# Softmax reciprocals as a power of minus one on GpSimd, and history copies on GpSimd, in a two-branch attention kernel

**The chip, the cores and the metric.** One core of one Trainium2 chip. The metric is the device time of the whole kernel in microseconds (us), the median of several executions; lower is better.

## The reference

Two attention branches share x (1 x 2048 x 640; 32 heads of 20). A is full softmax attention, B looks at a window of 8 positions two apart (its own and 7 earlier ones); a sigmoid gate mixes them. Cut to what matters:

```python
def _A_ref(x, wqkv, wo):            # full attention; B_ref is alike, over a window of 8 positions, 2 apart
    ...
    scores = jnp.einsum("bhqd,bhkd->bhqk", q, k) * scale
    p = _softmax(scores, axis=-1)
    o = jnp.einsum("bhqk,bhkd->bhqd", p, v)
    ...
g = _sigmoid((x * gate_w).sum(-1, keepdims=True))
return g * a + (1 - g) * b
```

## The kernel before

A runs in 32 groups (4 blocks of 512 queries, 8 sets of 4 heads). In each, TensorE makes score tiles, ScalarE takes the exponential of most of them (`ebuf`), and VectorE approximates it for the rest by integer arithmetic (`uD`, then shifted copies `eD` that TensorE weighs with `vS`). TensorE sums both into the PSUM bank `obank`; one row for each head holds the softmax denominator. At the end of a group the result is normalised:

```python
def gen_norm(g):
    qc, q = GROUPS[g]
    T("dve", dvc(512), lambda e: e.transpose(oTt[:, :], obank[:, :]), reads=["obank"], writes=["oTt"])
    while not done.get(("gate", qc)):
        yield ("cond",)
    yield ("dve",)
    T("dve", 0.25, lambda e: e.reciprocal(rcp[:, :], oTt[:, 0:512:32]), reads=["oTt"], writes=["rcp"])
    en, c1, c2 = ("dve", 0.12, dvc(512)) if g == NG - 1 else ("pool", 0.24, 1.08)
    T(en, c1, lambda e: e.tensor_tensor(rcp[:, :], rcp[:, :], gA[qc % 2][:, :], ALU.mult), ...)
    ...
    T(en, c2, lambda e: e.tensor_tensor(oo, ii, ib, ALU.mult), reads=["rcp", "oTt"], writes=["oN0"])
    yield ("dve", DVE_AHEAD, max(sch.ready("oN0"), sch.free("oN1")))
    T("dve", dvc(256), lambda e: e.transpose(oN[1]..., oN[0]...), reads=["oN0"], writes=["oN1"])
    if g < NG - 1:
        ... # small DMAs: oTd <- oN1, which a later output product reads
```

`T(engine, cost, instruction, ...)` enters an instruction into a scheduler that runs **while the kernel is built**. It keeps a clock for each engine, adds the cost given (in us), and so decides in which order the instructions stand on each engine; `yield` lets other work go first until the moment asked for. A table `PLAN` of some fifty rows of constants steers these decisions. Each engine of the chip is given its instructions in that order.

In branch B, k and v are kept with 16 columns of history ahead of them, copied from the end of the chunk before (`TB` enters VectorE work and adds it to B's progress):

```python
TB(0.15, lambda e, bb=bb: e.tensor_copy(bb[:, :, 0:PADB], bb[:, :, TOK:TOK + PADB]), reads=[key], writes=[key], port=True)
```

## Time and profile before

| | before |
|---|---|
| median time | 836.07 us (835.97 to 836.23, 3 runs) |
| ScalarE busy | 803.9 of 835.4 us |
| ScalarE idle: ends / inside its stream of exponentials | 22 / 9.5 us |
| TensorE busy / VectorE busy / GpSimd busy | 789.3 / 683.7 / 138.7 us |
| VectorE's waits for oN (the product made on GpSimd) | 4.6 us in 6 |

The prediction shows the lines that these come from, but for the last:

```profile
DVE oN L772 <- POOL oN L770: 4.6, 6, 1.4
```

One more view of the kernel before: the timeline of VectorE and GpSimd at one normalisation (start, duration, engine, line, operation, in us).

```profile
404.47 0.70 DVE L758 STREAM_TRANSPOSE oTt<-obank 128x512 f32<-128x512 f32 x1
405.21 0.25 DVE L762 RECIPROCAL rcp<-oTt 128x16 f32<-128x16 f32 x1
...
405.54 0.23 POOL L764 TENSOR_TENSOR rcp<-rcp,gA 128x16 f32<-128x16 f32 x1 [23.07 <-DVE rcp L762]
405.85 1.05 POOL L770 TENSOR_TENSOR oN<-oTt,rcp 128x512 bf16<-128x512 f32 x1
...
407.58 0.44 DVE L772 STREAM_TRANSPOSE oN<-oN 128x256 f32<-128x256 f32 x1
```

The path from the end of the first transpose (405.17) to the end of oN (406.90) is 1.73 us. The second transpose starts at 407.58 without waiting, 0.68 us later: the order has three other VectorE instructions ahead of it. Over all 31 places the kept trace gives 0.10 to 3.1 us between the end of oN and the second transpose, with a median of 0.67.

### The profile page before, as it was taken

What the parts mean: (1) busy time and instruction counts of PE and PEld (TensorE: products, weight loads), DVE (VectorE), ACT (ScalarE), POOL (GpSimd) and SP (SyncE); (2) the same over time, 40 slices, a digit from 0 to 9 for tenths busy, and PEclk for the clock granted to TensorE, in tenths of its full rate; (3) what the DMA queues carried; (4) which work ended last, traced back from release to release, by engine and by line L of the source; (5) the groups of instructions that cost most, each with busy time, mean ns of one, the idle gap of its engine ahead of it and who ended that gap; (6) DMA issues with size and microseconds to landing.
All of it is one profiled execution on the core that took longest, in us unless ns stands there. A gap on an engine that the chain in (4) does not pass through costs nothing.

```text
span 835.4 us, 29602 instructions
## 1 busy us (share of the span) xinstructions
PE 789.3 (94%) x12599; PEld 289.9 (35%) x12601; DVE 683.7 (82%) x1205; ACT 803.9 (96%) x767; POOL 138.7 (17%) x180
## 2 busy tenths in 40 slices
PE   8999999999999899989998999999999999998997
PEld 4333323334333332333233333333333333333223
DVE  7567888889888887978797988798898898887873
ACT  4999999999999999999999999999999999999994
POOL 5013013431111111011111011111102111101110
PEclk9999999999999999999999999999999999999999
DMA  9112112200111110011001011110011001101100
GB/s 313 30 37 44 33 25 45 73 13 19 29 37 29 29 30 20 7 42 32 20 18 41 18 20 29 36 42 9 5 39 30 10 20 25 38 6 31 32 6 34
DMA packets 45016, 29.15 MB, mean 35 GB/s; under 512 B 27204, under 2 KB 43684, under 8 KB 44884
## 3 DMA queue, kind: packets, MB, share of 16 engines
q1 hardware_dynamic: 44596, 26.92, 12.4%
q8 instruction: 100, 1.64, 0.8%
q10 hardware_dynamic: 288, 0.33, 0.1%
q14 instruction: 32, 0.26, 0.1%
HBM read 11.94 MB, written 2.62 MB: 17 GB/s over the span
## 4 chain that ended last, share of the span: by engine, by line
PE 54%; ACT 30%; issue 10%; DVE 5%; DVEq 0%; ACTq 0%
ACT ebuf L1538 30%; PE score L1515 17%; PE obank L1583 13%; PE side L557 13%; PE score L557 5%; PE obank L1604 2%; DVE uD L1528 1%; PE side L1604 1%; DVE eD L797 1%; PE obank L459 1%; PE score L1230 1%; PE side L885 1%; DVE stage L869 0%; PE score L1604 0%; DVE stage L970 0%
## 5 line engine op out<-in xcount | busy, mean ns | idle before, releaser
L1538 ACT ACTIVATE ebuf<-score 128x1024 bf16<-128x1024 f32 (+1 forms) x735 | 792.6, 1237 | 11.6 <-PE score L1515 9.7
L1515 PE MATMUL score<-qT,kT 32*128 32x512 bf16 x2048 | 291.9, 384 | 31.6 <-ACT ebuf L1538 20.6
L1528 DVE TENSOR_SCALAR uD<-score 128x512 int16<-128x512 f32 x324 | 217.2, 683 | 38.4 <-PE score L1515 36.1
L797 DVE TENSOR_SCALAR eD<-uD 128x2048 int16<-128x2048 int16 x243 | 168.1, 722 | 7.9 <-PE obank L1583 7.2
L1515 PEld LDWEIGHTS score<-qT,kT 32*128 32x128 bf16 x2048 | 75.1, 91 | 282.7 <-ACT ebuf L1538 137.6
L1583 PE MATMUL obank<-ebuf,vA 128*21 128x512 bf16 x1724 | 161.3, 385 | 2.2 <-ACT ebuf L1538 1.8
L789 POOL TENSOR_TENSOR vS<-vA,vw 128x252 bf16<-128x252 bf16 x81 | 61.0, 757 | 291.5 <-PE obank L1583 256.3
L557 PE MATMUL side<-xT,kvw 128*32 128x256 bf16 (+1 forms) x2530 | 103.0, 281 | 3.1 <-DVE qkvB L853 1.4
L1583 PE MATMUL obank<-eD,vS 128*21 128x512 bf16 x972 | 84.1, 382 | 0.0
L557 PEld LDWEIGHTS side<-xT,kvw 128*32 128x32 bf16 x2530 | 59.3, 96 | 37.9 <-issue 22.0
L764 POOL TENSOR_TENSOR rcp<-rcp,gA 128x16 f32<-128x16 f32 x31 | 11.3, 365 | 351.9 <-DVE rcp L762 351.9
L1583 PEld LDWEIGHTS obank<-ebuf,vA 128*21 128x21 bf16 x1724 | 38.6, 89 | 82.3 <-issue 69.5
L970 DVE TENSOR_TENSOR stage<-qkvB,repB 128x1280 bf16<-128x1280 bf16 x64 | 52.9, 856 | 0.7 <-DMA repB<-eB 0.7
L869 DVE TENSOR_TENSOR stage<-qkvB 128x1280 bf16<-128x1280 bf16 x64 | 51.4, 830 | 0.1
L853 DVE CAST qkvB<-side 128x512 bf16<-128x512 f32 (+1 forms) x72 | 41.9, 591 | 10.5 <-PE side L557 10.5
L557 PE MATMUL side<-stage,ident 128*32 128x512 bf16 (+1 forms) x736 | 47.4, 345 | 1.2 <-DVE uD L744 0.5
L1604 PE MATMUL obank<-xT,zero 128*32 128x512 bf16 x444 | 37.9, 385 | 0.0
L770 POOL TENSOR_TENSOR oN<-oTt,rcp 128x512 bf16<-128x512 f32 x31 | 33.0, 1065 | 2.4
L1583 PE MATMUL obank<-uD,vA 128*21 128x512 bf16 x324 | 31.7, 382 | 0.0
L758 DVE STREAM_TRANSPOSE oTt<-obank 128x512 f32<-128x512 f32 x32 | 22.7, 709 | 9.0 <-PE obank L1583 8.9
L1583 PEld LDWEIGHTS obank<-eD,vS 128*21 128x21 bf16 x972 | 24.0, 92 | 17.4 <-issue 4.1
L557 PE MATMUL side<-woA_d,oTd 128*32 128x128 bf16 (+1 forms) x580 | 28.8, 293 | 0.0
(173 smaller groups left out, 555.5 us busy)
## 6 DMA issues: line engine op xcount, KB each, us to landing
repB<-eB SPq DMA_DIRECT2D x128, 32.0 KB
WqP<-in_A_wqkv_dram SPq DMA_DIRECT2D x16, 160.0 KB
stage<-in_B_wqkv_dram SPq DMA_DIRECT2D x1, 2400.0 KB
oTd<-oN SPq DMA_DIRECT2D x108, 20.0 KB
qT<-dst SPq DMA_DIRECT2D x104, 20.0 KB
out_dram<-outsb SPq DMA_DIRECT2D x12, 160.0 KB
kvw<-in_A_wqkv_dram SPq DMA_DIRECT2D x2, 800.0 KB
oTd<-in_A_x_dram SPq DMA_DIRECT2D x2, 640.0 KB
```

What stands on the lines that cost most here:

```text
L557: ins = e.matmul(o[j:k, :], l(j) if callable(l) else l[:, j:k], r, start=(first and i == 0), stop=(last and i == n - 1), skip_group_check= ...
L770: T(en, c2, lambda e: e.tensor_tensor(oo, ii, ib, ALU.mult), reads=["rcp", "oTt"], writes=["oN0"])
L789: T("pool", 0.7, lambda e: e.tensor_tensor(vS[:, d % 2, :, :], _ap(vA, (kb * NQ + q) * 4 * DV, [[0, K - 1], [1, 4 * DV]]), _ap(vw, 0, [[1, ...
L797: T("dve", 0.11 + 0.1334 * n, lambda e, k=k, sl=sl: e.tensor_scalar(eD[:, sl % NS, 0:512 * n].bitcast(I16), uD[d % 2][:, 0:512 * n].bitcas ...
L853: t = TB(dvc(n * TOK), lambda e, o=o, i=i: e.tensor_copy(o, i), reads=[("side", b)], writes=[key])
L869: TB(dvc(CN * TOK, 2), lambda e, w=w, ks=ks: e.tensor_tensor(prodB(w), qB[:, :, :], ks, ALU.mult), reads=["qB", "kB"], writes=[("prod", w) ...
L970: TB(dvc(CN * TOK, 2), lambda e, w=w, vs=vs, rr=rr: e.tensor_tensor(prodB(w), vs, rr, ALU.mult), reads=["vB", ("repB", w4 % NR)], writes=[ ...
L1515: ins = e.matmul(o, kT[32 * j:32 * j + 32, q, kb * P:(kb + 1) * P], qT[g % NQT][32 * j:32 * j + 32, :], start=True, stop=True)
L1528: t = T("dve", 0.69, lambda e: e.tensor_scalar(uD[d % 2][:, 512 * i:512 * (i + 1)].bitcast(I16), side[x], UOFF, 0.0, op0=ALU.add, op1=ALU. ...
L1538: exps[s] = T("act", actc(512 * n), lambda e: e.activation(ebuf[s % NE][:, 0:512 * n], score[s % 2][:, 0:512 * n], ACTF.Exp, scale=LN2 / S ...
L1583: ins = e.matmul(obank[32 * j:32 * j + DV, :], v, src, start=(kb == 0), stop=(last and k >= len(lst) - 4), skip_group_check=True)
L1604: ins = e.matmul(o[32 * j:32 * j + 32, :], w[:, 32 * j:32 * j + 32] if best else w[:, :], xT[:, 0, 0:512], start=bool(best), stop=bool(bes ...
```

## The change

The change takes work off VectorE: 31 of 32 reciprocals become a power with exponent -1 on GpSimd, ahead of the gate's product that was there already, and the 14 history copies go to GpSimd. `PLAN` is replaced by another table, and `BALL`, the total against which B's progress is measured, is lowered by 2. The diff, with all but the first of the 49 old and 54 new rows of the table cut:

```diff
 PLAN = {
-    0: ((0.34, 0.64), 0.37, 6.3, 2.5, 0.51, -1.0, -0.1, 11.8, 4.5, 7.2, 0.52, 0.47, 4.4, 1.86, 0.0, 0.85, 2, 0.0),
+    0: ((0.3, 0.64), 0.32, 2.5, 2.5, 0.49, -1.0, -0.1, 11.8, 7.0, 7.2, 0.51, 0.34, 4.4, 4.0, 0.0, 0.81, 2, 0.0),
 ... (all other rows: cut)
+    minus1 = sb([P, 1], FP32, "minus1")
...
+        T("dve", 0.06, lambda e: e.memset(minus1[:, :], -1.0), writes=["minus1"])
...
-        yield ("dve",)
-        T("dve", 0.25, lambda e: e.reciprocal(rcp[:, :], oTt[:, 0:512:32]), reads=["oTt"], writes=["rcp"])
+        if g == NG - 1:
+            yield ("dve",)
+            T("dve", 0.25, lambda e: e.reciprocal(rcp[:, :], oTt[:, 0:512:32]), reads=["oTt"], writes=["rcp"])
+        else:
+            T("pool", 0.8, lambda e: e.tensor_tensor(rcp[:, :], oTt[:, 0:512:32], _ap(minus1, 0, [[0, 16]]), ALU.pow),
+              reads=["oTt", "minus1"], writes=["rcp"])
...
-                TB(0.15, lambda e, bb=bb: e.tensor_copy(bb[:, :, 0:PADB], bb[:, :, TOK:TOK + PADB]), reads=[key], writes=[key], port=True)
+                T("pool", 0.3, lambda e, bb=bb: e.tensor_copy(bb[:, :, 0:PADB], bb[:, :, TOK:TOK + PADB]), reads=[key], writes=[key])
...
-    BALL = 172.0
+    BALL = 170.0
```

## The prediction

> **What bounds the kernel now.** I read the page first (busy times), then the ScalarE groups by form, the ScalarE part of the waits, and the ScalarE timeline at the two ends.
>
> Busy times and the chain of the page:
>
> ```profile
> PE 789.3 (94%) x12599; PEld 289.9 (35%) x12601; DVE 683.7 (82%) x1205; ACT 803.9 (96%) x767; POOL 138.7 (17%) x180
> ...
> PE 54%; ACT 30%; issue 10%; DVE 5%; DVEq 0%; ACTq 0%
> ```
>
> ScalarE (ACT) is busy 803.9 of 835.4 us, so it is idle for only 31.5 us in the whole run. TensorE's 94% is softer than it looks. The kernel puts in matmuls that compute nothing, where the build-time scheduler sees TensorE idle: line 1604, 444 of them into obank and 304 more into the other banks, 748 in all. They run four at a time, so they make 187 slots of about 0.215 us (the spacing of such slots in the timeline), some 40 us of work that could be left out. VectorE (DVE), which the change relieves, has 152 us of idle time and holds 5% of the chain.
>
> ScalarE's groups by form, and who ended its waits:
>
> ```profile
> L1538 ACT ACTIVATE ebuf<-score 128x1024 bf16<-128x1024 f32 x479 | 463.4, 1082 | 6.4 <-PE score L1515 5.0
> L1538 ACT ACTIVATE ebuf<-score 128x1536 bf16<-128x1536 f32 x255 | 359.2, 1530 | 5.1 <-PE score L1515 4.4 <-ACT ebuf L1538 0.2
> ```
> ```profile
> ACT ebuf L1538 <- PE score L1515: 9.7, 24, 2.1
> ACT stage L1082 <- PE score L1063: 6.9, 1, 6.9
> ACT xT L1243 <- PE score L1230: 6.3, 3, 4.4
> ```
>
> The exponentials of A's scores fill ScalarE. The reader is to see how little it waits in that stream: 9.7 us in 24 waits, all for score tiles from TensorE. The rest of its idle time lies at the ends. The timeline shows both: the first exponential starts at 19.62, the last starts at 823.22 and takes 0.60, and the end follows from 823.8 to 835.4 without an exponential.
>
> ```profile
> 19.62 1.45 ACT L1538 ACTIVATE ebuf<-score 128x1536 bf16<-128x1536 f32 x1 [2.10 <-PE score L1515]
> ...
> 823.22 0.60 ACT L1538 ACTIVATE ebuf<-score 128x512 bf16<-128x512 f32 x1 [0.18 <-PE score L1515]
> ...
> 830.75 1.08 ACT L1082 ACTIVATE stage<-score 128x512 bf16<-128x512 f32 x2 [6.93 <-PE score L1063]
> ```
>
> Up to 19.62 ScalarE works about 8.1 us and idles 11.5. After 823.8 it works 1.1 and idles 10.5. So 22 of the 31.5 idle us are the fixed ends, and **9.5 us is the idle time inside the stream**. That 9.5 us is all that a lighter VectorE can win.
>
> **What the Trainium skill says.** (1) "SBUF — State Buffer", section "SBUF: two separate sides": GpSimd and VectorE share one port pair as an exclusive lock; a VectorE instruction in a two-port mode, or with two SBUF inputs against a GpSimd one that reads SBUF, and a GpSimd instruction shut each other out for a whole instruction. The trace agrees: vS on GpSimd takes 598 to 1191 ns, and the VectorE eD instruction 627 to 1860. (2) "GPSIMD Engine Reference", section "Engine selection": elementwise work is about twice as slow there for two inputs. The trace has the same two steps on both engines: 128x16 multiply 222 ns (GpSimd, undisturbed) against 175, and the scaling of oN 1052 against 751; so 1.3 to 1.4 here. (3) "VectorE: DVE Perf Modes", section "Walkthrough: the 8-slice pipeline in each mode": VectorE's reciprocal is an iterated hardware divide, not a plain stream. The trace: 243 ns for 128x16, 68 more than the multiply of the same shape. No page that I found gives the cost of a power on GpSimd, and no row of this trace has one.
>
> **The change, part by part.**
>
> ```profile
> L758 DVE STREAM_TRANSPOSE oTt<-obank 128x512 f32<-128x512 f32 x32 | 22.7, 709 | 9.0 <-PE obank L1583 8.9
> L762 DVE RECIPROCAL rcp<-oTt 128x16 f32<-128x16 f32 x32 | 7.8, 243 | 0.4
> L840 DVE COPY qkvB<-qkvB 128x80 bf16<-128x80 bf16 x14 | 2.4, 173 | 0.1
> L764 POOL TENSOR_TENSOR rcp<-rcp,gA 128x16 f32<-128x16 f32 x31 | 11.3, 365 | 351.9 <-DVE rcp L762 351.9
> L770 POOL TENSOR_TENSOR oN<-oTt,rcp 128x512 bf16<-128x512 f32 x31 | 33.0, 1065 | 2.4
> ```
>
> *Removed from VectorE:* 31 of 32 reciprocals, 31 x 0.243 = 7.5 us, and all 14 history copies, 2.4 us: 9.9 us together. The gate's product was on GpSimd before already; what moves is the reciprocal ahead of it.
>
> *Added on GpSimd:* 31 powers and 14 copies. The scheduler's own entries for GpSimd (0.24 for the product, 1.08 for oN, 0.7 for vS) are close to what the trace has (0.222, 1.052, 0.610), so its entries for the new steps are probably measured too: 0.8 and 0.3. That is 31 x 0.8 + 14 x 0.3 = 29 us more, 138.7 to about 167 of 835: no bound. The path from oTt to oN grows: at 405 us of the timeline it is 0.25 (reciprocal) + 0.08 + 0.23 + 0.08 + 1.05; the power puts 0.8 where 0.25 was, so oN is 0.6 us later. The transpose that uses it is placed by the scheduler, which counts on this, so little of it should be waited for.
>
> *Given back through the lock:* two-port and two-input VectorE instructions start 243 + 64 + 64 times in 835 us, 0.45 per us. A power of 0.8 us meets 0.36 of them and holds each back by half its length at most on average: 31 x 0.36 x 0.4 = 4.5 us of VectorE time, an estimate, and the copies add 14 x 0.13 x 0.15, nothing. So of 9.9 us some 5.5 stays won.
>
> *The whole order is made anew.* This is the larger part. A table of scheduling constants is replaced, and the listings of the two built programs differ almost everywhere. Counts in them: exponentials of 1024 go 479 to 472, of 1536 from 255 to 261; score tiles that VectorE converts (uD) 324 to 320, the shifts eD 243 to 240; matmuls that compute nothing 748 to 804, so 14 more slots. The relief of VectorE was thus not spent on taking work from ScalarE: four more score tiles go through ScalarE. By the busy share of one (463.4/479 = 0.967 and 359.2/255 = 1.409 us, overlaps counted once) that is 6 x 1.409 - 7 x 0.967 = **+1.7 us of ScalarE**. VectorE gets 4 x 0.67 + 3 x 0.69 = 4.7 us less in addition. The listings of the first instructions and of the last (final tiles, output products, four final adds) are alike but for small shifts, so the 22 us of the ends stay.
>
> *Sum:* time = ends and other ScalarE work as before + 1.7 + the stream's idle time. With the stream's idle time unchanged at 9.5 that is 836.1 + 1.7 = 837.8. With none left it would be 828.3. How much of it goes? The waits of TensorE show what held the score tiles up:
>
> ```profile
> PEld score L1515 <- DVE uD L1528: 24.4, 53, 0.9
> PEld score L1515 <- DVE eD L797: 12.4, 32, 0.6
> PEld score L1515 <- DVE oTt L758: 4.3, 7, 0.9
> PEld score L1515 <- DVE rcp L762: 3.5, 7, 0.8
> ```
>
> VectorE is what TensorE waited for after ScalarE itself (137.6 us, which is harmless), and TensorE seldom lets ScalarE run dry: some of the ScalarE gaps that I opened in the timeline (305.77, 458.42) have score matmuls delayed by a run of obank work, others (452.67, 692.37, 715.51) follow a run of VectorE evacuations. About 45% of 9.5 us, 4.3 us, is my choice: a lighter VectorE, and an order that was tuned for it. That gives 837.8 - 4.3 = **833.5 us**.
>
> **Rivals.** *(a) The saving is hidden and the new order costs.* VectorE is not the bound, so nothing is won, and 1.7 us of ScalarE comes on top: 837.8, or up to 842 if the new order fits the chip less well than the old one. For it: 5% of VectorE in the chain, and the count of exponentials went up. Against: an order worse than the old one would hardly have been kept. *(b) A new wait on GpSimd.* The power takes 2 us, not 0.8; oN then comes 1.2 us late 31 times and VectorE, which works in order, waits for it. Before there is a trace of it: "DVE oN L772 <- POOL oN L770: 4.6, 6". Up to 31 x 1.2 = 37 us of VectorE waiting, against 152 us of idle time; a quarter of it reaching ScalarE makes 845. Likewise 8 of VectorE's conversions into qkvB now wait for a GpSimd copy; if that stands behind a vS that waits for TensorE, VectorE stands still. The scheduler puts vS in only when its buffer is about to come free, which speaks against long waits. *(c) The order fits much better*, nearly all of the 9.5 us goes and fewer TensorE stalls occur: 829 to 830.
>
> **Range and chances.** Main line 830 to 836, (a) 837 to 842, (b) 840 to 850, (c) 829. With 55, 25, 8 and 12 in a hundred the middle is 833.5 and 828.5 to 840.0 holds about eight in ten. Faster by over 2% needs 819.3, below the 828.3 of a ScalarE that never waits in its stream, so only if fixed ends shrink: 0.02. Slower by over 2% needs 852.8, only a bad (b): 0.03. Within 2%: 0.95.
>
> **What would show it.** ScalarE busy about 805.6; VectorE busy about 669 to 674 (683.7 - 9.9 - 4.7 and up to 4.5 back); GpSimd 165 to 170 with the power at 0.7 to 0.9 us; the ends 19.6 and 11.6 us long as before; ScalarE's waits for score tiles in the stream some 5 us in place of 9.7. Rival (a) shows as waits of 9 us or more there with VectorE lighter all the same; (b) as VectorE's waits for oN or the copies above 10 us; (c) as waits under 2 us. I would be wrong in kind if the ends moved by more than 2 us, or if VectorE's busy time did not fall.

## The result, and the profile after

The changed kernel takes **867.34 us** (867.07 to 870.48, 4 runs) against 836.15 (4 runs of the kernel before): ratio 1.0379, 95% interval 1.0354 to 1.0404. It is 31 us slower, and outside the range predicted. A ratio here is the mean time of one kernel's runs over the mean of the other's from the same rounds, so not quite the quotient of the medians quoted.

Busy times and chain on the page of the changed kernel:

```profile
PE 802.2 (93%) x12645; PEld 291.0 (34%) x12645; DVE 665.5 (77%) x1154; ACT 810.8 (94%) x766; POOL 225.5 (26%) x224
...
PE 46%; ACT 22%; DVE 13%; POOL 9%; issue 7%; SPq 2%; DMA 1%; DVEq 0%; ACTq 0%; POOLq 0%
```

ScalarE has 6.9 us more work and is idle for 54.6 us in place of 31.5. VectorE is lighter, as expected, yet its share of the chain went from 5% to 13%, and GpSimd, which was not in the chain, has 9%. So the path that ended last now runs through these two more than before. The group of the power, from the page, and the main waits (who waited for whom: total us, times, longest):

```profile
L772 POOL TENSOR_TENSOR rcp<-oTt,minus 128x16 f32<-128x16 f32 x31 | 91.2, 2944 | 296.0 <-DVE oTt L765 281.1
```
```profile
DVE oN L783 <- POOL oN L781: 60.5, 27, 4.3
PEld score L1526 <- DVE uD L1539: 41.0, 69, 1.9
ACT ebuf L1549 <- PE score L1526: 33.4, 51, 2.3
```

Read the last three from the top. A power takes 2.9 us, not 0.8. VectorE, which works in order, stands for 60.5 us at the second transpose (4.6 before). Behind it stand the evacuations of score tiles that TensorE waits for (41.0, was 24.4), and ScalarE runs dry 51 times for 33.4 us (24 times, 9.7). One normalisation in the timeline, all engines in order of start:

```profile
491.51 0.71 DVE L765 STREAM_TRANSPOSE oTt<-obank 128x512 f32<-128x512 f32 x1
...
492.30 2.90 POOL L772 TENSOR_TENSOR rcp<-oTt,minus 128x16 f32<-128x16 f32 x1 [0.86 <-DVE oTt L765]
...
495.58 1.05 POOL L781 TENSOR_TENSOR oN<-oTt,rcp 128x512 bf16<-128x512 f32 x1
...
496.73 0.45 DVE L783 STREAM_TRANSPOSE oN<-oN 128x256 f32<-128x256 f32 x1 [2.94 <-POOL oN L781]
497.10 0.65 DVE L1539 TENSOR_SCALAR uD<-score 128x512 int16<-128x512 f32 x1
...
497.81 0.60 PE L1526 MATMUL score<-qT,kT 32*128 32x512 bf16 x3 [0.81 <-DVE uD L1539]
...
498.51 8.16 ACT L1549 ACTIVATE ebuf<-score 128x1024 bf16<-128x1024 f32 x7 [1.25 <-PE score L1526]
```

The whole chain of events is in these lines: VectorE idle for 2.94 us, then the evacuation it held up, then the score matmul that needed the evacuated bank, then a ScalarE gap of 1.25 us. Of 2.94 us of VectorE's standstill 1.25 reached the engine that bounds the kernel. Over the whole run the books close: ScalarE's busy time grew by 6.9 us and its waits in the stream by 23.7 (33.4 - 9.7), against a span 30.0 us longer (865.4 - 835.4).

### The profile page after: what moved, and what is told of

Its sections match the earlier page's. It is cut to its first block, busy times and chain, and to the rows that moved or that the text cites. A ratio compares the mean times of both kernels' runs of the same rounds, so it can differ in the third digit from the quotient of the medians.

```text
span 865.4 us, 29697 instructions
## 1 busy us (share of the span) xinstructions
PE 802.2 (93%) x12645; PEld 291.0 (34%) x12645; DVE 665.5 (77%) x1154; ACT 810.8 (94%) x766; POOL 225.5 (26%) x224
## 3 DMA queue, kind: packets, MB, share of 16 engines
q8 instruction: 100, 1.64, 0.8%
## 4 chain that ended last, share of the span: by engine, by line
PE 46%; ACT 22%; DVE 13%; POOL 9%; issue 7%; SPq 2%; DMA 1%; DVEq 0%; ACTq 0%; POOLq 0%
ACT ebuf L1549 22%; PE score L1526 14%; PE side L564 11%; PE obank L1594 11%; POOL rcp L772 6%; PE score L564 4%; DVE uD L1539 3%; POOL oN L781 2%; DVE oTt L765 2%; DVE eD L808 1%; SPq L711 1%; DVE stage L880 1%; PE obank L1615 1%; DVE stage L981 1%; PE score L1615 1%
## 5 line engine op out<-in xcount | busy, mean ns | idle before, releaser
L1549 ACT ACTIVATE ebuf<-score 128x1024 bf16<-128x1024 f32 (+1 forms) x734 | 798.9, 1205 | 35.4 <-PE score L1526 33.4
L1526 PE MATMUL score<-qT,kT 32*128 32x512 bf16 x2048 | 296.0, 388 | 33.1 <-ACT ebuf L1549 17.4
L772 POOL TENSOR_TENSOR rcp<-oTt,minus 128x16 f32<-128x16 f32 x31 | 91.2, 2944 | 296.0 <-DVE oTt L765 281.1
L800 POOL TENSOR_TENSOR vS<-vA,vw 128x252 bf16<-128x252 bf16 x80 | 57.6, 724 | 217.8 <-PE obank L1594 182.6
L564 PE MATMUL side<-xT,kvw 128*32 128x256 bf16 (+2 forms) x2480 | 101.4, 280 | 3.3 <-DVE qkvB L864 2.1
L564 PEld LDWEIGHTS side<-xT,kvw 128*32 128x32 bf16 (+1 forms) x2480 | 57.5, 96 | 39.2 <-issue 21.3
L783 DVE STREAM_TRANSPOSE oN<-oN 128x256 f32<-128x256 f32 x32 | 14.2, 444 | 60.8 <-POOL oN L781 60.5
L564 PE MATMUL side<-stage,ident 128*32 128x512 bf16 (+1 forms) x704 | 44.4, 343 | 1.0 <-DVE qbnd L698 0.7
L564 PE MATMUL side<-woBp,oB 128*32 128x128 bf16 (+1 forms) x540 | 25.8, 295 | 5.3 <-DVE oB L998 2.4
L1615 PE MATMUL obank<-xT,zero 128*32 128x512 bf16 x364 | 30.0, 385 | 0.0
```

The lines of the kernel that those rows point to most:

```text
L564: ins = e.matmul(o[j:k, :], l(j) if callable(l) else l[:, j:k], r, start=(first and i == 0), stop=(last and i == n - 1), skip_group_check= ...
L772: T("pool", 0.8, lambda e: e.tensor_tensor(rcp[:, :], oTt[:, 0:512:32], _ap(minus1, 0, [[0, 16]]), ALU.pow), reads=["oTt", "minus1"], writ ...
L800: T("pool", 0.7, lambda e: e.tensor_tensor(vS[:, d % 2, :, :], _ap(vA, (kb * NQ + q) * 4 * DV, [[0, K - 1], [1, 4 * DV]]), _ap(vw, 0, [[1, ...
L1526: ins = e.matmul(o, kT[32 * j:32 * j + 32, q, kb * P:(kb + 1) * P], qT[g % NQT][32 * j:32 * j + 32, :], start=True, stop=True)
L1549: exps[s] = T("act", actc(512 * n), lambda e: e.activation(ebuf[s % NE][:, 0:512 * n], score[s % 2][:, 0:512 * n], ACTF.Exp, scale=LN2 / S ...
L1615: ins = e.matmul(o[32 * j:32 * j + 32, :], w[:, 32 * j:32 * j + 32] if best else w[:, :], xT[:, 0, 0:512], start=bool(best), stop=bool(bes ...
```

## The experiments

**Theory 1:** the power is longer than the order counts on, the path from oTt to oN is late, and VectorE stands at the second transpose. **Theory 2:** the new order (a new `PLAN`, more exponentials) or the history copies cost the time. **Theory 3:** the power costs by its load: it holds the port that GpSimd and VectorE share, or makes `vS` late behind it on GpSimd.

Because the scheduler makes a different order as soon as a cost changes, most experiments keep the costs it reckons with and alter only what is emitted, so that every other instruction stands where it stood. The diffs below are shortened, and comments in them are added for the reader. The median of the kernel before, run beside them on the same chips, was 836.86 us (runs 1 to 4), 837.07 (5 to 7) and 837.37 (8 and 9).

| run | time, us | ratio to before (95%) | VectorE's waits for oN | ScalarE's waits for scores in the stream |
|---|---|---|---|---|
| changed kernel | 867.34 | 1.0379 (1.0354 to 1.0404) | 60.5 | 33.4 |
| 1 cheap product for the power | 839.12 | 1.0026 (1.0003 to 1.0050) | 5.0 | 10.8 |
| 2 half the columns a power | 845.94 | 1.0112 (1.0094 to 1.0131) | 32.4 | 14.7 |
| 3 second transpose later | 860.17 | 1.0289 (1.0249 to 1.0330) | none | 28.4 |
| 4 idle power in the old path | 885.54 | 1.0584 (1.0541 to 1.0627) | 70.0 | 54.6 |
| 5 reciprocal on VectorE again | 839.61 | 1.0032 (1.0017 to 1.0046) | 4.8 | 10.7 |
| 6 only the copies moved | 836.18 | 0.9997 (0.9982 to 1.0011) | 4.2 | 11.9 |
| 7 idle power off the path | 838.29 | 1.0015 (1.0001 to 1.0030) | 4.6 | 11.0 |
| 8 scheduler told 2.98 us | 892.63 | 1.0662 (1.0640 to 1.0684) | 30.7 | 24.8 |
| 9 control of 4 | 838.50 | 1.0011 (0.9993 to 1.0029) | 8.1 | 12.9 |

### 1. A cheap product in place of the power, same order (wrong output on purpose)

```diff
-            T("pool", 0.8, ... _ap(minus1, 0, [[0, 16]]), ALU.pow),
+            T("pool", 0.8, ... _ap(minus1, 0, [[0, 16]]), ALU.mult),     # and minus1 holds 1e-35
```

> The changed kernel in the very same order of instructions, with the power of 2.90 us replaced by a multiplication by a tiny constant of the same shape (wrong output on purpose). Theory 1 (the length of the power): the product takes about 0.22 us, VectorE's waits for oN fall from 60.5 us to under 10, and the time falls from 867 to 834 to 838 us, about the kernel before. Theory 2 (the new order, or the history copies on GpSimd, fit the chip worse, and the power is only a bystander): 858 us or more.

Measured: 839.12 us. From the view of the tile rcp (duration min/median/max in ns) and the waits:

```profile
L772 POOL TENSOR_TENSOR rcp<-oTt,minus x31: 219/223/746, 57.5 to 804.1; 128x16 f32<-128x16 f32 x31
```
```profile
ACT ebuf L1549 <- PE score L1526: 10.8, 19, 2.2
...
DVE oN L783 <- POOL oN L781: 5.0, 4, 1.7
```

28 of the 31 us are gone with the length of one operation. (The values computed changed too; run 5, with the right output, takes the same time.) The median is 1 us above the band that theory 1 gave. Theory 2 is refuted as the cause; what is left for the new order and the copies together is 0.26%, some 2 us.

### 2. Half the columns as a power, same order (wrong output on purpose)

```diff
-            T("pool", 0.8, lambda e: e.tensor_tensor(rcp[:, :], oTt[:, 0:512:32], _ap(minus1, 0, [[0, 16]]), ALU.pow),
+            T("pool", 0.8, lambda e: (e.tensor_tensor(rcp[:, 0:8], oTt[:, 0:256:32], _ap(minus1, 0, [[0, 8]]), ALU.pow),
+                                      e.tensor_tensor(rcp[:, 8:16], oTt[:, 256:512:32], _ap(tiny, 0, [[0, 8]]), ALU.mult))[1],
```

> The same order again, with 8 of the 16 columns as a power and the other 8 as the cheap product (wrong output on purpose). If the power costs by the element, its instruction takes about half of 2.90 us plus a fixed part, 1.5 to 1.6 us, and with the 0.3 us of the extra product the path is about 1.1 us shorter: 845 to 853 us. If it is a fixed cost of the operation, it stays near 2.8 us and the time at 865 or more.

Measured: 845.94 us, in the band of a cost by the element.

```profile
L773 POOL TENSOR_TENSOR rcp<-oTt,minus x31: 1633/1637/2175, 58.2 to 809.8; 128x8 f32<-128x8 f32 x31
```
```profile
DVE oN L785 <- POOL oN L783: 32.4, 19, 3.2
```

The power takes 1.637 us for 8 columns and 2.900 for 16: (2.900 - 1.637) / 8 = 0.158 us a column and 2.900 - 16 x 0.158 = 0.37 us fixed. The time of the kernel is not linear in that length. From the start of the replaced instruction to the start of the gate's product the traces have 0.30 us in run 1, 1.88 here and 2.98 in the changed kernel (medians of 31):

| | path longer, 31 places | VectorE's waits for oN | time |
|---|---|---|---|
| from run 1 to here | 31 x 1.58 = 49.0 us | +27.4 us | +6.8 us |
| from here to the changed kernel | 31 x 1.10 = 34.1 us | +28.1 us | +21.4 us |

So two things take up delay. In the first step nearly half of it never becomes a wait of VectorE: it falls into slack like the 0.68 us shown above. And of the wait that does arise, a quarter reaches the time in the first step and three quarters in the second. After the first step each us of delay costs 21.4 / 34.1 = 0.63 us. What holds the wait off ScalarE at first was not looked into.

### 3. The second transpose later, power as it is (right output)

```diff
+    lst = sch.lists["dve"]                 # after the order is made, before it is emitted
+    for t in moved:                        # the 31 transposes of oN
+        i = lst.index(t)
+        stop = min([lst.index(h) for h in heads if lst.index(h) > i])   # not past the next transpose of obank
+        lst.insert(min(i + 5, stop - 1), lst.pop(i))
```

> The changed kernel with the power as it is and a right output; only the 31 transposes of oN stand five instructions later in VectorE's order, some 3.3 us of its work. Theory 1 in its narrow form (VectorE, which works in order, stands at the transpose and waits for oN): its waits for oN fall from 60.5 us to under 10 and the time to 836 to 842 us, with the power still 2.90 us. If the power hurts in another way (it shuts VectorE out of the shared port, or makes vS late on GpSimd), the time stays above 855 us. Theory 2: no change, 865 or more.

Measured: 860.17 us (858.0 to 865.8). The step "VectorE no longer waits for oN" came true completely, and the gain of 7 us was far from the 25 or more expected. So the narrow form of theory 1 fell. The timeline shows what took the place of the wait in the longest gap: the consumer of the transpose's result.

```profile
826.40 0.43 DVE L784 STREAM_TRANSPOSE oN<-oN 128x256 f32<-128x256 f32 x1
...
831.89 1.90 PE L564 MATMUL side<-woBp,oB 128*32 128x512 bf16 x16 [4.36 <-DMA oTd<-oN]
...
834.43 1.45 ACT L1551 ACTIVATE ebuf<-score 128x1536 bf16<-128x1536 f32 x1 [5.13 <-PE score L1528]
```

The DMAs that spread oN leave later, the output product that reads them stands at the head of TensorE's order and waits 4.36 us (its first matmuls, which name the row, are B's, on oB; the step as a whole waits for oTd), and ScalarE runs dry for 5.13. The four longest gaps of this run, 12.6 of the 28.4 us, all stand behind a transfer of the queue that SyncE issues. The other three are 3.15 us at 340.67 (VectorE's qbnd step waited 2.24 for qT), 2.55 at 308.51 (VectorE waited 2.75 for repB) and 1.77 at 103.59 (a score matmul waited 1.98 for qT), and ahead of each the transfers of oTd stand in that queue (from 324.13, 297.34 and 94.40). So in these four the delay of the path appears to be passed on from one engine working in order to the next; the shorter gaps were not opened.

### 4. An idle power in the kernel before, in the path (right output)

```diff
-        T(en, c1, lambda e: e.tensor_tensor(rcp[:, :], rcp[:, :], gA[qc % 2][:, :], ALU.mult), ...
+        product = lambda e: e.tensor_tensor(rcp[:, :], rcp[:, :], gA[qc % 2][:, :], ALU.mult)
+        T(en, c1, product if g == NG - 1 else lambda e: (
+            e.tensor_tensor(unused[:, :], oTt[:, 0:512:32], _ap(minus1, 0, [[0, 16]]), ALU.pow), product(e))[1], ...
```

> The kernel before in its very same order, reciprocal and copies on VectorE, with an additional power of oTt on GpSimd ahead of the gate's product, whose result nobody uses (right output). Theory 1: oN comes 2.9 us later than the order counts on, so VectorE waits some 50 to 80 us for it and the time rises from 836 to 860 to 875 us, without a new order and without GpSimd copies. Theory 2: 836 to 840 us.

Measured: 885.54 us, above the band, in the direction of theory 1. The old order, with reciprocals and copies on VectorE, loses 49 us when oN comes 2.9 us late, with waits of the same kinds as in the changed kernel.

```profile
DVE oN L776 <- POOL oN L774: 70.0, 30, 4.2
ACT ebuf L1542 <- PE score L1519: 54.6, 76, 2.3
```

That it is more than 31 us goes with the delay: here all of the 2.87 us that the power puts ahead of the gate's product is unforeseen, in the changed kernel some 2.1 of its 2.98. The sizes were not worked out from this.

### 5. The reciprocal on VectorE again, order of the changed kernel (right output)

```diff
+        def both(e, g=g):
+            e.transpose(oTt[:, :], obank[:, :]).then_inc(inner, 1)
+            e.wait_ge(inner, g + 1)
+            return e.reciprocal(rcp[:, :], oTt[:, 0:512:32])
...
-            T("pool", 0.8, lambda e: e.tensor_tensor(rcp[:, :], ... ALU.pow), reads=["oTt", "minus1"], writes=["rcp"])
+            T("pool", 0.8, lambda e: e.memset(unused[:, :], 0.0), reads=["oTt", "minus1"], writes=["rcp"])
```

> The changed kernel in its own order, the history copies on GpSimd, but the 31 reciprocals on VectorE again: each stands directly behind the transpose that makes oTt, in the same step of the order, and GpSimd clears one unused column where the power was (right output). It is the cheap-product run with 7.5 us more on VectorE. If VectorE's 7.5 us are worth nothing, because it is not the bound: 837 to 840 us, the same as the cheap product within 1.5 us. If they are worth what I chose in the prediction (about half): 841 to 844.

Measured: 839.61 us with VectorE at 676.1 us busy, against 839.12 with 669.0 for the cheap product. In ratios to before they are 1.0032 and 1.0026, with overlapping intervals. The time is in the first band that was given. The 7 us of VectorE that the power was to save are worth nothing that could be measured.

### 6. Only the copies, order of the kernel before (right output)

```diff
+    for t in moved:                        # the 14 copies
+        sch.lists["dve"].remove(t)
+        t.stream = "pool"
+        pl = sch.lists["pool"]
+        pl.insert(next((i for i, x in enumerate(pl) if x.idx > t.idx), len(pl)), t)
```

> The kernel before in its own order with the second part of the change alone: the 14 history copies on GpSimd, at the same place in the order (right output). VectorE loses 2.4 us of work and is not the bound, and GpSimd does a copy in 0.25 us: the same time within 1.5 us, 834.5 to 838. If VectorE's conversions into qkvB come to wait for copies that stand behind other GpSimd work, some 2 us or more slower.

Measured: 836.18 us, ratio 0.9997. The second part of the change neither helps nor hurts.

### 7. The idle power off the path (right output)

```diff
+        def product(e):
+            p = e.tensor_tensor(oo, ii, ib, ALU.mult)          # makes oN, and signals it
+            if g < NG - 1:
+                e.tensor_tensor(unused[:, :], _ap(two, 0, [[0, 16]]), _ap(minus1, 0, [[0, 16]]), ALU.pow)
+            return p
```

> The kernel before in its own order with the same 31 idle powers as in the run that took 885 us, but behind the product that makes oN in place of ahead of the gate's product, and with constants as input, so that nothing waits for their results (right output). If the power hurts only as latency between oTt and oN: 836 to 842 us, with VectorE's waits for oN at the 5 us of before. If it hurts by its load, because it holds the port that GpSimd and VectorE share or makes vS late: 855 us or more.

Measured: 838.29 us. From the view of the tile that the power writes, and the waits:

```profile
L776 POOL TENSOR_TENSOR unused<-two,minus x31: 2888/2895/3836, 60.0 to 805.1; 128x16 f32<-128x16 f32 x31
```
```profile
DVE oN L781 <- POOL oN L774: 4.6, 6, 1.4
```

The same 31 powers, behind the two products in GpSimd's order, cost 1.2 us in place of 49. Theory 3 is refuted as the main cause: neither the 90 us of additional GpSimd load nor the shared port does the damage; the latency does. VectorE's busy time rose by 2.8 us (683.7 to 686.5), which may be the lock: by the trace, ten of the VectorE instructions that take over 0.1 us longer than their kind alone ran beside a power. One reserve: this power read a constant tile, the other the 128x16 columns of oTt; the duration is the same.

### 8. The scheduler told the right length (right output)

```diff
-            T("pool", 0.8, lambda e: e.tensor_tensor(rcp[:, :], ... ALU.pow),
+            T("pool", 2.98, lambda e: e.tensor_tensor(rcp[:, :], ... ALU.pow),
```

> The changed kernel with one number changed in what the scheduler reckons with: 2.98 us for the power in place of 0.8 (right output). The scheduler then makes a wholly different order, with the table of constants left as it was. If the loss is only that the scheduler was told too short a time, the order now leaves room for the power: VectorE's waits for oN below 15 us and the time 836 to 845 us. If the table fits only the course it was found for, or the longer path itself costs, then VectorE's waits for oN are gone all the same but the time is not won back: 860 us or more.

Measured: 892.63 us, the slowest of all. VectorE's waits for oN halved (30.7 us in 11) but did not go, so both expectations missed there; the time went where the second one said. The busy times of its page tell where:

```profile
PE 828.6 (93%) x13073; PEld 305.3 (34%) x13073; DVE 619.0 (69%) x1077; ACT 827.6 (93%) x786; POOL 218.8 (25%) x213
```

By the listing of the built program, the new order gives VectorE only 276 score tiles in place of the 324 of before, so ScalarE does 48 more and is busy for 827.6 us, 23.7 more than before; and in the last 73 us of the run it works 43. After its last exponential it stands for one wait of 25.6 us, 6.9 before:

```profile
ACT stage L1093 <- PE side L1074: 25.6, 1, 25.6
```

With its waits in the stream (24.8 against 9.7) this makes up the whole difference: 23.7 + 18.7 + 15.1 = 57.5 us, and the span is 57.5 longer. So the largest part is the share of work that the new order gives ScalarE, and a third of it is the end. That the table of constants, found for another course of events, steers badly once the course changes is the likely reason; it was not tested. A table found anew for the right length was not run, so whether the power can be used without loss in a better order stays open.

### 9. Control of 4: an idle product in the path (right output)

```diff
-            e.tensor_tensor(unused[:, :], oTt[:, 0:512:32], _ap(minus1, 0, [[0, 16]]), ALU.pow), product(e))[1], ...
+            e.tensor_tensor(unused[:, :], oTt[:, 0:512:32], _ap(minus1, 0, [[0, 16]]), ALU.mult), product(e))[1], ...
```

> Control of the run that put an idle power ahead of the gate's product in the kernel before and took 885 us: the same program with an idle multiplication of the same shape there (right output). If the length counts, and not the additional instruction: 0.3 us longer a path, 836 to 840 us. If an additional instruction there costs as such: 850 or more.

Measured: 838.50 us. The additional instruction as such costs nothing that could be measured; the longer path (the gate's product 2.87 us behind its start there, 0.18 here) costs 47 us (885.54 - 838.50). No experiment gave a kernel faster than the one before by more than noise.

## Why the prediction was wrong

**The step that failed is the cost of the power.** The prediction found no row of the trace and no page with it, and took the scheduler's entry: "its entries for the new steps are probably measured too: 0.8 and 0.3". The copy was fairly near (0.25 us measured without disturbance). The power was 2.90, 3.6 times its entry. From this followed "oN is 0.6 us later", where the removed reciprocal and its gap (0.33) stand against 2.98: 2.65 us later; and "the scheduler ... counts on this, so little of it should be waited for", where 2.1 us of each were not counted on. In place of "little" VectorE waited 60.5 us for oN, 4.6 before, and ScalarE 33.4 us for score tiles, 9.7 before. Agreement of three known entries with the trace said nothing of the one entry that no trace had.

**Rival (b) had the mechanism, with too little weight and too short a power.** It put the power at 2 us, so 37 us of VectorE waiting and 845. Run 2 happens to be that case: the gate's product 1.88 us behind the start of the power, 32.4 us of waiting, 845.94 us; there its "quarter of it reaching ScalarE" held as well (6.8 of 27.4), which was chosen and not worked out. At the real length 2.1 us are unforeseen, 31 x 2.1 = 65 us of waiting; 60.5 was measured, and the share no longer held: the loss of the power is 867.3 - 839.1 = 28 us, half of the 55.5 us of waiting that it added (60.5 - 5.0). The slack at 404 to 408 us of the profile before, 0.68 us, could have warned that a delay of 2 us is not absorbed by it. The rival got 8 in a hundred; an operation whose duration nobody had seen, placed in a path with an in-order engine waiting at its end, deserved more. The other wait that the rival named, VectorE's conversions behind GpSimd's copies, is not among the longer waits of the changed kernel, and run 6 has no loss from it.

**The gain of 4.3 us did not come.** With the power out of the way (runs 1 and 5) ScalarE's waits for score tiles are 10.8 and 10.7 us, where "some 5 us" was predicted and 9.7 was the value before. This is rival (a): relieving VectorE, which was not the bound, gave nothing. The 4.3 had been a choice, not a sum. Run 6 says the same of the copies.

**The +1.7 us of ScalarE was about right.** Run 1 has ScalarE at 806.6, 2.7 more than before, and the time is up by about 2.2 (0.26%), which is rival (a)'s 837.8 within noise. The changed kernel has 6.9 more; run 4, with the same exponentials as the kernel before, also has 7.0 more (810.9). Waits (51 and 76 against 24) break up exponentials whose records otherwise overlap, which is a likely reason for the rest, but it was not tested.

**The ends held:** the first exponential at 19.60 us, and 11.0 us after the last one. **VectorE's busy time fell** to 665.5, 3.5 below the band of 669 to 674: the term that the lock was to give back had the wrong sign. The kept traces show it in four kinds of VectorE instructions (eD, qabs and the two stage products). None of them that runs without GpSimd beside it is over 0.02 us longer than the median of such ones of its kind in the kernel before; those that overlap a GpSimd instruction add up to 16 us above it before, 11 in the changed kernel and 19 in run 7. Eleven of the long ones before ran beside the product that makes oN, none after: there VectorE stands and waits for that product. That run 4, with as many powers, also lowers VectorE's busy time (to 674.6) agrees with this.

**GpSimd** was to reach 165 to 170 us and reached 225.5: 91.2 of it are the power, where 25 had been reckoned.

**Open.** The granted TensorE clock was 0.983 to 0.986 in the changed kernel (0.998 before) and 0.970 to 0.980 in run 4. Run 1, in the same order, has 0.996 to 1.000, so the lower clock comes with the late path; by which way is not shown, and the share of the 31 us that comes through it was not separated. The 25 runs of the kernel before that stand beside the experiments give a measure: at 0.999 and 1.000 they took 834.9 to 836.3 us (one 837.9), at 0.994 and 0.995 837.5 to 839.7, and a straight line through all gives some 0.6 us for each 0.001. If that held between kernels, it would be some 7 of the 31 us, an estimate. Between 300 and 400 us the clock was 1.00 and ScalarE still idled 4.2 us (0.4 before), so part of the loss arises without it.

## What to carry to other kernels

Moving work off an engine that was not the bound won nothing here (runs 1, 5 and 6), and where the new place lay in a dependency path, most of its latency counted once the slack was used (0.63 us for each us, run 2 against the changed kernel): measure an operation's duration on the target engine before building an order around it. The same load can cost 49 us or 1 us depending on whether something in order waits for it; ask of every moved instruction who waits for it and how long that one can stand idle. In a kernel whose order is computed from costs, keep the order fixed and alter only what is emitted when a cause is to be found, since a corrected cost changed everything at once (run 8).

## What the Trainium skill lacked or had wrong

- No page that I found gives the duration of a power on GpSimd. The runs show 2.90 us for 128x16 and 1.64 us for 128x8 in fp32, about 0.158 us a column and 0.37 fixed (runs 1 and 2 and the changed kernel), against 0.22 us for a product and 0.24 to 0.25 for VectorE's reciprocal of the same shape. "GPSIMD Engine Reference", section "Engine selection", has about 2x for elementwise work with two inputs; here it is 1.3 to 1.4 for the product and about 12 for a reciprocal made this way.
- "Perfetto Trace Analysis", section "GPSIMD Engine Instruction", has it that GpSimd's spans in a profile are unreliable and that the spacing of starts should be used. For the power the two agree: a span of 2.90 us, and the product starts 2.98 us after it (492.30 and 495.28 in the timeline).
- "SBUF — State Buffer", section "SBUF: two separate sides", describes the port lock and gives no price for a stream of short GpSimd instructions beside a busy VectorE. Run 7 shows it: 90 us of powers added 2.8 us to VectorE's busy time and 0.15% to the kernel's. It depends on what runs beside them: in run 4, with the same powers in the path, VectorE's busy time fell by 9.1 us.
